# The block matrix of a linear attention loaded in two halves, and the work in a new order

## The chip, the cores and the metric

The kernel runs on one core of a Trainium2 chip. Its metric is the device time of one execution in microseconds (us). The kernel before takes 259.46 us, the median of three runs (258.75 to 259.86).

The engines have these names in the profile: PE is TensorE (PEld its loading of weights), DVE is VectorE, ACT is ScalarE, POOL is GpSimd, SP is SyncE. SPq and ACTq are the instructions with which SyncE and ScalarE issue DMAs.

## The reference

Two layers follow each other. The first is a linear attention with a feature map that takes products of two small projections; the second normalizes, and is a gated linear unit.

```
phi(x) = outer(S1 x, S2 x), flattened             # 8 x 8 = 64 features of 32 numbers
kv = sum over s of phi(k_s) v_s^T ; z = sum over s of phi(k_s)
attn = phi(q) kv / (phi(q) z + 1e-6)              # 4 batches, 4 heads, 1088 tokens, head 32
x = attn as 4352 tokens x 128
xn = x / sqrt(mean(x^2) + 1e-6) * rms_g
out = (silu(xn w_gate) * (xn w_val)) w_out        # 128 -> 1536 -> 128
```

S1, S2 and the three weights arrive as 64-bit numbers, and the kernel turns their bits into 32-bit floats itself.

## The kernel before, in words

**Stages.** S1 and S2 stand in one block matrix `sw` for the four heads, 128 x 64 numbers of 8 bytes, 64 KB. One DMA on ScalarE's queue brings it to `s_raw`. Six small instructions (lines 371 to 389: absolute value, sign, low bits, clamp, shift, join) make `sblk` of it, and each product with keys or queries needs `sblk`. Keys come by batch in two pieces, values in two or three. For a batch the kernel computes the projections of the keys (L485), copies half of each out of PSUM (L309), multiplies them to `phi` (L439) and sums `phi` times the values (L497) into `kv`. Queries come in nine chunks of up to 512 tokens. For the first two chunks the projections (L550) are multiplied token by token (tile `at`), turned by TensorE (L558) and copied to `phiq`; the later ones go through DRAM (`far`, `at`, `bt`). Then `phiq` times `kv` (L627), a division, a norm and another turn (L675) give x in two parts, `x_hi` and `x_lo`.

**Slots.** For each chunk and each of 12 slices of 128 hidden columns there is a slot: three passes for the gate and three for the value (L726, high and low parts of weights and x), silu on ScalarE (L735), product on VectorE (L738, tile `h`), its high part on ScalarE (L753), its low part on VectorE or GpSimd (L756), three passes with the output weights (L764). A slice of the weights is 384 KB, loaded at L412 and converted by lines 346 to 423 for its first use; the tiles are `w_raw`, `w_tmp`, `w_f`, `w_hi` and `w_lo`.

**Order.** Every piece of work is a task in a plan, numbered as it is added. `ORDER` is a list of all the numbers, written out, and `ON` gives, letter by letter, the engine of each task that more than one engine can do (a, d, p for ScalarE, VectorE, GpSimd). `follow` goes through `ORDER`, gives each task a planned start from clocks of its own, and `run` emits the work sorted by that planned start. A DMA that ScalarE issues has a fixed planned start (`since`) and takes nothing of SyncE's clock; a DMA without `since` takes the next place on SyncE's clock, one `ISSUE` after the one before it in the list. Within an engine the instructions run as emitted. Up to `RING` = 8 DMAs are in flight; the ninth waits on its queue for the landing of the first.

The tasks at the start, by number before the change: 0 S, 1 ScalarE's table load (a silu of four numbers), 2 to 7 the six instructions of S, 8 and 9 copies of `sblk`, 10 and 11 the first keys in two pieces (256 KB and 320.5 KB), 13 and 14 the first queries in two halves of 128 KB, 15 to 17 values, 18 to 20 the first projection of keys with its copy and product, 36 to 39 the projection of the first half of queries, its copy, its product and its turn, 41 to 44 the same for the second half. After the change S is tasks 0 and 1, and every other number is one higher.

`SLATE` is a planned delay of S's landing that the plan adds to the others.

Of the kernel before, what the change touches and what calls it, by code (L numbers as in the profile page):

```python
# [12 lines left out]
U32 = mybir.dt.uint32  # L13
# [9 lines left out]
P = 128  # L23
# [5 lines left out]
HALF = 64  # L29
# [55 lines left out]
"""  # L85
# [16 lines left out]
SWITCH = 98  # L102
RING, ISSUE, FAR, FLIGHT, SETTLE = 8, 470, 640, 1650, 250
STALLS = ((4500, 600), (12000, 400))
SLATE = 650


class Buf:
# [760 lines left out]
```

## Time and profile before

| | |
|---|---|
| median of three runs | 259.46 us |
| profiled execution, its own time | 258.33 us |
| its span (first to last instruction) | 256.5 us |
| TensorE busy | 252.0 us (98%) |
| VectorE busy | 168.6 us (66%) |
| ScalarE busy | 153.8 us (60%) |
| GpSimd busy | 90.6 us (35%) |
| granted TensorE clock | 1.00 |

A row of the chain of waits has a start, a duration (both us) and what filled it: an engine with tile and line, a DMA, or "issue". A row of the timeline begins in the same way and has the engine, the line, the operation, the tile written and the tiles read, and in brackets the idle time of the engine before it with what ended it. A row of the table by stretches has its ends, its length, and the busy time and number of instructions of PE, PEld, DVE, ACT and POOL, then the granted clock, the DMA engines' busy share and GB/s. A row of groups has a count, the busy time, the mean in ns, the idle time before them and what ended it.

### The profile page before, as it was taken

The page shows a single profiled execution, that of the slowest core. Times are in us where ns is not written, and L with a number is a line of the kernel's source. Part 1 is how long each engine was busy: PE and PEld are TensorE (multiplying, and loading weights), DVE is VectorE, ACT ScalarE, POOL GpSimd, SP SyncE. Part 2 cuts the span into 40 slices and gives each one's busy share as a digit, 9 for nine tenths or more (in the row PEclk, how much of TensorE's full clock was granted, in tenths as well). Part 3 has the DMA queues.
Part 4 walks back from the last instruction along what each step waited for, and adds up shares of the span by engine and source line. Part 5 has one row for each costly group of instructions (what it writes and reads, how often), then busy time and mean ns, then how long its engine had stood idle before and what let it go on. Part 6 is the DMA issues. An engine that isn't in the chain of part 4 may idle for free.

```text
span 256.5 us, 5598 instructions
## 1 busy us (share of the span) xinstructions
PE 252.0 (98%) x2116; PEld 204.0 (80%) x2116; DVE 168.6 (66%) x390; ACT 153.8 (60%) x339; POOL 90.6 (35%) x92
## 2 busy tenths in 40 slices
PE   7999999999999999999999999999999999999995
PEld 5888777788887787788887888888888887888895
DVE  2998999989866676646464666647644554635643
ACT  3789888647664744575555555455556655554572
POOL 3444222123755412583516503145223714132031
PEclk9999999999999999999999999999999999999999
DMA  7999886064015115061320120001000100100010
GB/s 236 380 382 279 251 236 208 0 158 130 1 59 149 65 47 139 0 185 43 92 75 3 42 78 15 0 1 43 0 0 0 41 4 0 41 0 3 0 42 20
DMA packets 13498, 22.13 MB, mean 86 GB/s; under 512 B 1952, under 2 KB 5024, under 8 KB 13472
## 3 DMA queue, kind: packets, MB, share of 16 engines
q1 hardware_dynamic: 13040, 21.52, 27.0%
q8 instruction: 16, 0.26, 0.4%
q10 hardware_dynamic: 432, 0.26, 0.3%
q14 instruction: 10, 0.08, 0.1%
HBM read 18.69 MB, written 3.08 MB: 85 GB/s over the span
## 4 chain that ended last, share of the span: by engine, by line
PE 95%; ACT 2%; DMA 1%; POOL 1%; DVE 0%; issue 0%
PE g_ps L726 28%; PE v_ps L726 28%; PE o_ps L764 28%; PE att L627 3%; PE att L497 2%; PE att L675 2%; DMA s_raw<-sw 1%; PE att L485 1%; PE att L578 1%; PE o_ps L497 1%; ACT phiq L309 0%; ACT w_tmp L362 0%; POOL at L439 0%; PE att L745 0%; PE g_ps L485 0%; PE g_ps L558 0%
## 5 line engine op out<-in xcount | busy, mean ns | idle before, releaser
L738 DVE TENSOR_TENSOR h<-v_ps,s 128x512 f32<-128x512 f32 (+2 forms) x110 | 69.9, 649 | 49.7 <-PE v_ps L726 25.7
L756 POOL TENSOR_TENSOR h_lo<-h,h_hi 128x512 fp32r<-128x512 f32 (+1 forms) x43 | 53.0, 1242 | 109.2 <-DVE h_lo L756 39.7
L735 ACT ACTIVATE s<-g_ps 128x512 f32<-128x512 f32 (+1 forms) x108 | 60.8, 574 | 39.8 <-PE g_ps L726 32.7
L753 ACT CAST h_hi<-h 128x512 fp32r<-128x512 f32 (+1 forms) x106 | 61.3, 599 | 38.6 <-DVE h L738 35.5
L756 DVE TENSOR_TENSOR h_lo<-h,h_hi 128x512 fp32r<-128x512 f32 (+1 forms) x63 | 40.8, 660 | 13.4 <-ACT h_hi L753 10.0
L726 PE MATMUL g_ps<-x_hi,w_hi 128*128 128x512 f32 (+1 forms) x110 | 42.5, 387 | 0.0
L726 PE MATMUL v_ps<-x_hi,w_hi 128*128 128x512 f32 (+1 forms) x110 | 42.3, 385 | 0.0
L726 PE MATMUL g_ps<-x_lo,w_hi 128*128 128x512 f32 (+1 forms) x110 | 41.6, 379 | 0.0
L726 PE MATMUL v_ps<-x_hi,w_lo 128*128 128x512 f32 (+1 forms) x110 | 41.6, 378 | 0.0
L726 PE MATMUL g_ps<-x_hi,w_lo 128*128 128x512 f32 (+1 forms) x110 | 41.5, 378 | 0.0
L726 PE MATMUL v_ps<-x_lo,w_hi 128*128 128x512 f32 (+1 forms) x110 | 41.5, 379 | 0.0
L764 PE MATMUL o_ps<-h_hi,w_hi 128*128 128x512 f32 (+1 forms) x106 | 41.3, 389 | 0.0
L764 PE MATMUL o_ps<-h_hi,w_lo 128*128 128x512 f32 (+1 forms) x106 | 40.7, 384 | 0.0
L764 PE MATMUL o_ps<-h_lo,w_hi 128*128 128x512 f32 (+1 forms) x106 | 40.6, 383 | 0.0
L726 PEld LDWEIGHTS g_ps<-x_hi,w_hi 128*128 128x128 f32 x110 | 20.7, 188 | 4.8 <-ACT s L735 0.2
L726 PEld LDWEIGHTS v_ps<-x_hi,w_hi 128*128 128x128 f32 x110 | 20.7, 188 | 4.6 <-DVE h L738 0.3
L726 PEld LDWEIGHTS g_ps<-x_lo,w_hi 128*128 128x128 f32 x110 | 20.7, 188 | 4.2
L726 PEld LDWEIGHTS v_ps<-x_lo,w_hi 128*128 128x128 f32 x110 | 20.6, 188 | 4.2
L726 PEld LDWEIGHTS v_ps<-x_hi,w_lo 128*128 128x128 f32 x110 | 20.7, 188 | 4.0
L726 PEld LDWEIGHTS g_ps<-x_hi,w_lo 128*128 128x128 f32 x110 | 20.7, 188 | 3.9
L764 PEld LDWEIGHTS o_ps<-h_lo,w_hi 128*128 128x128 f32 x106 | 19.9, 188 | 4.3
L764 PEld LDWEIGHTS o_ps<-h_hi,w_hi 128*128 128x128 f32 x106 | 19.9, 188 | 4.1
(97 smaller groups left out, 256.5 us busy)
## 6 DMA issues: line engine op xcount, KB each, us to landing
w_raw<-w SPq DMA_DIRECT2D x12, 384.0 KB
bt<-far SPq DMA_DIRECT2D x24, 128.0 KB
at<-far SPq DMA_DIRECT2D x12, 256.0 KB
outT<-o_sb SPq DMA_DIRECT2D x8, 256.0 KB
q<-qT SPq DMA_DIRECT2D x7, 256.0 KB
vt<-v SPq DMA_DIRECT2D x4, 272.0 KB
kt<-kT SPq DMA_DIRECT2D x4, 256.0 KB
vt<-v SPq DMA_DIRECT2D x3, 340.0 KB
```

Of the source, the lines that this page charges most:

```text
L485: nc.tensor.matmul(out=ab()[n0:rows.stop, (t - lo) * HALF:(t - lo + 1) * HALF], lhsT=kt()[:, s0:s0 + len(rows)], rhs=sblk, start=True, sto ...
L497: nc.tensor.matmul(out=kvv[r0:r0 + wide, h // 2, :], lhsT=phi()[:, t, h * F + f:h * F + f + wide], rhs=vt()[:, t, h, :], start=(t == 0 and ...
L578: nc.tensor.matmul(out=accs[p]()[a * D:(a + 1) * D, :m], lhsT=sab[rows, p].rearrange("p c o r -> p (c o r)"), rhs=q()[rows, a * m:(a + 1) ...
L627: nc.tensor.matmul(out=nv[n0:rows.stop, t, p, :], lhsT=phi()[:, p, l0:l0 + len(rows)], rhs=kvs[cut][:, p, :], start=True, stop=True,)
L675: nc.tensor.transpose(out=xt()[:, t * P:(t + 1) * P], in_=xn()[:, t, :], identity=ident)
L726: nc.tensor.matmul(out=acc()[:, cs], lhsT=wt[:, j, i3, :], rhs=x()[:, cs], start=(i == 0), stop=(i == 2))
L735: act(n, lambda: nc.scalar.activation(out=s()[:, :n], in_=gps()[:, :n], func=AF.Silu), cols(gps, whole[0]), [s])
L738: cs.stop - cs.start, lambda cs=cs: nc.vector.tensor_tensor(out=h()[:, cs], in0=vps()[:, cs], in1=s()[:, cs], op=ALU.mult),
L753: act(n, lambda: nc.scalar.copy(out=h_hi()[:, :n], in_=h()[:, :n]), hs, [h_hi], True)
L756: eng.tensor_tensor(out=h_lo()[:, :n], in0=h()[:, :n], in1=h_hi().bitcast(F32)[:, :n], op=ALU.subtract)
L764: nc.tensor.matmul(out=o_ps()[:, :n], lhsT=wt[:, j, 2, :], rhs=x()[:, :n], start=first and i == 0, stop=last and i == 2,)
```

## The change

The change was announced as "S loaded in two halves, the first transfer of both queues; both halves of the first queries by ScalarE's queue; order searched anew". S is loaded by two DMAs of 64 partitions each: the first half on SyncE's queue, planned without `since`, the second on ScalarE's with `since` 740 as before. Both halves of the first queries are now issued by ScalarE, the second one 430 ns of the plan after the first; before, the second half was SyncE's. What reads S now waits for both halves. `SLATE` becomes 250 and counts for ScalarE's half alone. `ORDER` and `ON` are replaced as a whole; below stand their first lines. Among the tasks that change the engine are the absolute value of S (2 before, 3 after: a to d) and the products of the first queries (38 and 43 before: p and d; 39 and 44 after: d and p).

```diff
 ORDER = """
-1 0 2 3 5 4 10 6 7 18 19 20 14 41 42 43 13 36 11 68 15 37 79 38 22 23 26 30 31 16 24 17 212 32 69 12 27 207 9 208 28 39 80 44 45 8 21 25 29 33 209 213
...
+1 11 2 0 3 4 6 5 7 8 19 20 14 15 12 69 21 37 38 16 80 42 39 43 17 18 23 24 31 27 44 213 208 13 32 214 9 40 25 45 28 29 22 26 33 209 210 30 34 81 215
...
 ON = (
-    "aapddadapaaapaddaaaaaappapdadpapdapdadpadpapdapdaddappappadapadddapaddaaaapdddddaadapapdaaaddddaddddddadpdddddpppdpapdda"
...
+    "dapadddapaaadaapaaaaaappappadpadpappaddaddappadpaddadpappapapadaaadaapaaaapdddddaadadapdaaadpddaddddddaddddddppdddpadapa"
...
-SLATE = 650
+SLATE = 250
...
-    plan.add({"dma": Way(
-        ISSUE + SLATE, P * NB * 8 / 320, lambda: nc.scalar.dma_start(out=s_raw.rearrange("p n c -> p (n c)"), in_=sw.bitcast(U32)), since=740
-    )}, (), ["s_raw"])
+    for i, rows in enumerate((slice(0, HALF), slice(HALF, P))):
+        eng = nc.scalar if i else nc.sync
+        plan.add({"dma": Way(ISSUE + SLATE * i, HALF * NB * 8 / 320, lambda eng=eng, rows=rows: eng.dma_start(
+            out=s_raw[rows].rearrange("p n c -> p (n c)"), in_=sw.bitcast(U32)[rows]), since=740 * i)}, (), [("s_raw", i)])
...
-    plan.add({"act": on_act(NB, s_abs, True), "dve": on_dve(NB, s_abs_dve, fast=True)}, ["s_raw", "table"], ["s_tmp"])
-    dve(NB, s_side, ["s_raw"], ["s_top"], fast=True)
-    dve(NB, s_low, ["s_raw", "s_top"], ["s_top"], lock=True)
+    plan.add({"act": on_act(NB, s_abs, True), "dve": on_dve(NB, s_abs_dve, fast=True)}, [("s_raw", 0), ("s_raw", 1), "table"], ["s_tmp"])
+    dve(NB, s_side, [("s_raw", 0), ("s_raw", 1)], ["s_top"], fast=True)
+    dve(NB, s_low, [("s_raw", 0), ("s_raw", 1), "s_top"], ["s_top"], lock=True)
...
-            eng = nc.sync if c or i else nc.scalar
+            eng = nc.sync if c else nc.scalar
             load(
                 P * (hi - lo) * 4, lambda eng=eng, lo=lo, hi=hi: eng.dma_start(out=q()[:, lo:hi], in_=qT[:, s0 + lo:s0 + hi]), [(q, i)],
-                since=0 if c or i else 1170,
+                since=0 if c else 1170 + 430 * i,
             )
```

More of the change, by code (lines that the diff above doesn't have):

```diff
@@ L48 @@
 ORDER = """
[36 rows of a table removed]
[36 rows of a table added]
 """
 ON = (
-    "aapddadapaaapaddaaaaaappapdadpapdapdadpadpapdapdaddappappadapadddapaddaaaapdddddaadapapdaaaddddaddddddadpdddddpppdpapdda"
-    "paaaadpaaadpddppdppddpaaaddaaapppddpddddppaaadpdddpdpddpddddddadadpdddpdppddppdpdpdaappaaddpppppddpdpddadpddapdpdpddpddd"
-    "dadpdddppddpa"
+    "dapadddapaaadaapaaaaaappappadpadpappaddaddappadpaddadpappapapadaaadaapaaaapdddddaadadapdaaadpddaddddddaddddddppdddpadapa"
+    "pdaaapdaddpddddppddpdpaaapddaappdpdpdpddpdaaadpadddddppppdppppdddpdaddpdppdddppddpaaddpdaddpdddddpdddpdaddpadppppdppppdp"
+    "dadpppppddpda"
 )
```

70 rows, old and new, of the table ORDER are left out of this document.

## The prediction

> **What bounds the kernel now.** I read the page's chain of work that ended last first, by engine.
>
> ```profile
> PE 95%; ACT 2%; DMA 1%; POOL 1%; DVE 0%; issue 0%
> ```
>
> TensorE is 95% of the chain. So a change can gain only where TensorE still waits (the first 18 us, as I read it, and the end) or where it changes the shape of its matrices. The chain, read again for the first 26 us, shows what TensorE waits for there:
>
> ```profile
> 0.73 3.25 DMA s_raw<-sw
> ...
> 4.01 0.27 ACT s_tmp L379
> ...
> 4.30 0.20 DVE s_tmp L382
> ...
> 4.76 0.23 DVE sblk L389
> ...
> 5.04 0.36 PE g_ps L485 x4
> ...
> 7.43 0.66 PE g_ps L558 x4
> ...
> 14.02 0.31 ACT w_hi L420
> 14.33 0.22 ACT kab L309
> ...
> 17.67 0.43 PE v_ps L726 x2
> ...
> 24.11 0.89 PE v_ps L726 x3
> 25.00 0.70 PE g_ps L726 x3
> ```
>
> S lands at 0.73 + 3.25 = 3.98 us, becomes `sblk` 1.01 us later (4.76 + 0.23), and TensorE starts at 5.04. From there the chain is computing alone, down to the last product; no later DMA stands in it. What S gains or loses is handed on whole, until something else is late. Of the other waits one bears on the change, and it stands just ahead of the 7.43: TensorE waits there for a product of GpSimd (its row comes below). The last two rows give a price that I need below: three passes of 512 columns take 0.70 us, and 0.89 straight after matrices of another shape.
>
> **The change part by part.** The sum is made against the profiled execution (258.33 us, span 256.5); the median of the runs shown, 259.46, lies 1.13 above it, and I carry the same difference over to it.
>
> *S in two halves.* The diff gives the SyncE half (task 0) no `since`, so it takes the place that the list gives it on SyncE's clock, and the new list has 11, the first keys, ahead of 0. Emission goes by planned start. The SyncE half is therefore second on its queue, behind 256 KB, whatever the words that announce the change say; only the ScalarE half is first. The second place is where half of the first queries stood:
>
> ```profile
> 0.74 0.39 SPq L457 DMA_DIRECT2D kt<-kT  x1
> 1.19 0.41 SPq L524 DMA_DIRECT2D q<-qT  x1
> ...
> kt<-kT SPq DMA_DIRECT2D x1, 320.5 KB
> ...
> kt<-kT SPq DMA_DIRECT2D x1, 256.0 KB
> ...
> q<-qT ACTq DMA_DIRECT2D x1, 128.0 KB
> ...
> s_raw<-sw ACTq DMA_DIRECT2D x1, 64.0 KB
> ```
>
> How fast the bytes move, by stretches (the last column is GB/s):
>
> ```profile
> 1.50:2.00 0.50, 0.50 (x4) 0.25 (x2) 0.00 (x0) 0.34 (x1) 0.41 (x3) 1.00 0.59 66
> 2.00:2.50 0.50, 0.50 (x4) 0.32 (x3) 0.00 (x0) 0.50 (x1) 0.00 (x0) 1.00 0.57 174
> 2.50:3.00 0.50, 0.50 (x4) 0.31 (x3) 0.00 (x0) 0.49 (x2) 0.00 (x0) 1.00 1.02 371
> 3.00:3.50 0.50, 0.50 (x4) 0.25 (x2) 0.00 (x0) 0.16 (x1) 0.00 (x0) 1.00 1.07 367
> 3.50:4.00 0.50, 0.50 (x4) 0.25 (x2) 0.00 (x0) 0.00 (x0) 0.00 (x0) 1.00 1.17 348
> 4.00:4.50 0.50, 0.34 (x2) 0.00 (x0) 0.40 (x3) 0.26 (x1) 0.00 (x0) 1.00 0.94 335
> 4.50:5.00 0.50, 0.00 (x0) 0.00 (x0) 0.45 (x3) 0.00 (x0) 0.00 (x0) 1.00 1.12 332
> ```
>
> From 2.5 us on both queues together move 371 GB/s at most, so S's landing is set by how many bytes go before its last one. Before, these were S and the first keys (320 KB, 328 thousand bytes), and up to half of SyncE's queries (64 KB). Now they are again S and the keys, and between none and all of ScalarE's first queries (128 KB), which follow its half of S. The ends: 64 KB fewer than before, 65.5/369 = -0.18 us; 128 KB more, +0.35 us. I take the middle, **+0.08**. The Trainium skill speaks against this part (DMA: Bandwidth & Descriptors, Rules for kernel authors): two transfers to disjoint halves of the partitions serialize on the same engines, and one of 128 partitions is advised. By that rule this term would be 0 and the sum below -0.31; the rows above agree with it, in that two queues at once move no more than 371 GB/s.
>
> *The absolute value goes from ScalarE to VectorE* (first letter of `ON`). VectorE's twin of it, the instruction that starts at the same 4.01, takes 0.20 where ScalarE's took 0.26:
>
> ```profile
> 4.01 0.20 DVE L371 TENSOR_SCALAR s_top<-s_raw 128x64 uint32<-128x64 uint32 x1 [3.14 <-DMA s_raw<-sw]
> ...
> 5.66 0.29 DVE L310 COPY both<-att 128x128 f32<-128x128 f32 x1 [0.67 <-PE att L550]
> 5.99 0.69 DVE L439 TENSOR_TENSOR at<-att,both 128x512 f32<-128x512 f32 x1
> 6.59 0.35 DVE L310 COPY both<-v_ps 128x192 f32<-128x192 f32 x1
> ...
> 9.99 0.36 DVE L346 TENSOR_SCALAR w_tmp<-w_tmp 128x384 f32<-128x384 f32 x1 [0.20 <-POOL at L439]
> ```
>
> The next instruction, which waited for it, starts 4.30 -> 4.23: **-0.07**, with nothing else queued on VectorE then (it had been idle for 3.14 us). ScalarE's table load moves behind one DMA issue more (0.41 us, as at 1.19), and nothing on VectorE's way waits for it.
>
> *The second half of the first queries goes to ScalarE's queue, third there.* Its issue moves from 1.19 to about 1.6 (the diff's 1170 + 430 ns), and it can become the last of five transfers: S, both pieces of keys, both halves of queries, 896.5 KB or 918 thousand bytes. By the stretches 830 thousand have moved at 4.5 us and 918 at 4.76. S came 0.74 to 0.92 us after its bytes had been counted (3.24 or 3.06 to 3.98), so this half lands at 5.50 to 5.68 at worst. The new list uses it as TensorE's third piece of work, after half of these products, at 5.21 + 0.32 = 5.53:
>
> ```profile
> 5.21 0.64 PE L550 MATMUL att<-sblk,q 128*64 128x64 f32 x16
> ```
>
>  Ends 0 and +0.18; I take **0**, since a wait there stands in front of 7.2 us, where TensorE waits today anyway. The other transfers of SyncE keep their bytes ahead of them; with eight in flight, the first weights now wait for a landing (S's first half, before 4.05) where they were issued without a wait, but the DMA share is near 1 until 5 us by the rows above, so this is covered.
>
> *The engines of the first products change places.* Before, GpSimd multiplied the half that is turned first, and TensorE waited for it; now VectorE does (tasks 39 and 44 of the new list: d, p). The wait in question, and what follows from it on GpSimd and ScalarE:
>
> ```profile
> 7.43 0.42 PEld L558 LDWEIGHTS g_ps<-ident,at 128*128 128x128 f32 x4 [0.24 <-POOL at L439]
> ...
> 8.88 1.07 POOL L439 TENSOR_TENSOR at<-both 128x512 f32<-128x512 f32 x1 [0.48 <-PE v_ps L558]
> ```
>
> VectorE's product, begun at 5.99, is done by about 6.7, so the transposes start 0.24 earlier; GpSimd's is needed only by the second of them, 0.6 later. Behind it GpSimd's next product waits for these transposes, and VectorE's conversion of weights at 9.99 for that product: the **-0.24** is handed on. Three copies leave VectorE (the rows at 5.66 and 6.59, and the second chunk's, of the form of 5.66) and one of 192 columns comes: 0.29 + 0.35 + 0.29 - 0.35 = 0.58 us less work, of which I count nothing more, because the row at 9.99 waits for GpSimd and not for VectorE's queue. At the other end those 0.58 count beyond the 0.24, another -0.34. ScalarE takes the three copies over; the wait that covers them is ScalarE's own for the first weights, and a gap ahead of it:
>
> ```profile
> 6.82 0.27 ACT L309 COPY both<-v_ps 128x128 f32<-128x128 f32 x1 [0.67 <-PE v_ps L485]
> ...
> 8.69 0.56 ACT L362 ACTIVATE w_tmp<-w_raw 128x384 f32<-128x384 f32 x1 [0.41 <-DMA w_raw<-w]
> ```
>
> Together they hold 1.08 us, against three copies of 0.27 to 0.35, 0.9 at most, which is what they would cost without this cover.
>
> *ScalarE's order to the first slots.* A copy of `kab` (0.22 on the chain) moves behind the first x. Ends 0 and -0.22 - 0.31 (with a `w_hi` as well); I take about half of the first, **-0.10**.
>
> *The order after that.* The sets of work are the same and TensorE is full in both orders. Counted in the lists, its matrices change shape 43 times where it was 42: 0 to 0.19, I take **+0.10**. Other effects of the order I price at 0 and leave to the rivals.
>
> Sum: 0.08 - 0.07 + 0 - 0.24 - 0.10 + 0.10 = **-0.23 us**: 258.1 for the profiled execution, and about **259.2** for the median.
>
> **The rivals.** *S's own half behind the keys costs more than the rest gains (slower).* S lands at +0.35, TensorE starts at 5.04 + 0.35 - 0.07 = 5.32 and waits 0.18 for the late queries. The transposes then start 0.46 after the 7.19 at which they could have started before, at 7.65 instead of 7.43: +0.22, and with the 0.10 of shapes 259.8. It decides once S lands later than about 4.3. For it: 256 KB stand ahead of this half. Against it: its place held 128 KB that nothing waited for, and S needs 32 of them.
>
> *All the early terms come whole (faster).* -0.18 - 0.07 - 0.24 - 0.34 - 0.53 = -1.36: 258.1. For it: each term has its row above. Against it: TensorE's waits in that stage depend on several engines at once, and the next one steps in.
>
> *The change does what it was announced to do*, and the SyncE half goes out first. Then 256 KB fewer are ahead of S, 262/369 = -0.71 in place of +0.08: -1.02, 258.4. Against it stand the list and the missing `since`.
>
> *VectorE falls behind between 25 and 60 us (slower).* It is nearly full there:
>
> ```profile
> 40.00:60.00 20.00, 20.00 (x251) 15.97 (x250) 18.87 (x40) 12.31 (x29) 4.76 (x5) 1.00 0.45 133
> ...
> L738 DVE TENSOR_TENSOR h<-v_ps,s 128x512 f32<-128x512 f32 (+2 forms) x110 | 69.9, 649 | 49.7 <-PE v_ps L726 25.7
> L753 ACT CAST h_hi<-h 128x512 fp32r<-128x512 f32 (+1 forms) x106 | 61.3, 599 | 38.6 <-DVE h L738 35.5
> L756 DVE TENSOR_TENSOR h_lo<-h,h_hi 128x512 fp32r<-128x512 f32 (+1 forms) x63 | 40.8, 660 | 13.4 <-ACT h_hi L753 10.0
> L354 DVE SCALAR_TENSOR_TENSOR w_tmp<-w_raw,w_tmp 128x384 uint32<-128x384 uint32 x8 | 4.4, 550 | 0.8 <-POOL w_lo L423 0.8
> ```
>
> In the new list four products of 0.70 lie between the v product of the tightest slot there (index 16) and its o product, five before. The way through h, h_hi and h_lo takes 0.65 + 0.60 + 0.66 = 1.91 us, which leaves 0.9. If VectorE runs two long and two short conversions late (0.55 twice, 0.36 twice as at 9.99: 1.82), TensorE stands for 0.9 there, and for as long again at the next weights: +1.8, 261.0. It decides once VectorE is more than 0.9 us late there. Against it: no row of this stage shows TensorE waiting now, and the list moves four of the h_lo from VectorE to GpSimd.
>
> **How the numbers follow.** Forecast 0.50 (its own range, the ends of its single terms short of all coming together, 258.7 to 259.7), all early terms 0.18, announced order of the transfers 0.05, S late 0.14, VectorE behind 0.13. A measurement of this kernel can tell about 0.5%, 1.3 us, from no change: under 258.16 is faster, over 260.76 slower. Faster takes six tenths of the second case, a third of the third and a tenth of the forecast: 0.18. Slower takes most of the last, a little of S late and of the forecast: 0.13. The rest, 0.69, is the same. The range that holds eight in ten cuts the second and the last case in two: 258.0 to 260.7.
>
> **What would show it.** The ScalarE half and the SyncE half on their queues: second place for the latter, behind kt. S's last landing near 4.05 (rival: 3.8, 4.3, or 3.3) and TensorE's first product at 5.0. The transposes at about 7.2 with no wait for GpSimd. The first slot near 17.4 where it is 17.67, and from 25 us on a TensorE without waits. I am wrong if TensorE waits anywhere between 25 and 60 us, if the first product comes before 4.7, or if the start is as I say and the end is not.

## The result, and the profile after

The changed kernel takes 261.3 us (median of 14 runs, 259.48 to 262.5); the kernel before, beside it, 258.73 us (14 runs, 258.11 to 260.09). The ratio is 1.0085, with a 95% interval of 1.0061 to 1.011: slower, by 2.2 us (1.6 to 2.8). Forecast were 259.2 us, and 258.0 to 260.7 as the range. The profiled execution took 261.33 us (span 259.5), 3.0 us more than that of before.

First the chain of work that ended last, by engine over the whole span, and then the rows of its start:

```profile
PE 95%; DMA 2%; ACT 1%; ACTq 0%; issue 0%; DVE 0%
```

```profile
2.02 5.91 DMA q<-qT
...
7.97 0.70 PE att L551 x8
8.67 1.07 PE v_ps L486 x20
9.74 0.64 PE g_ps L486 x12
10.38 0.65 PE att L551 x16
11.03 0.59 PE g_ps L559 x4
```

Before, this chain began with S (0.73 + 3.25). Now it begins with the second half of the first queries: issued at 2.02 us as ScalarE's third transfer, it lands at 7.93, where the prediction had put 5.68 as the worst. The turn of the queries (L559, L558 before) stands at 11.03 instead of 7.43.

TensorE's rows of the timeline around the wait:

```profile
5.75 0.34 PE L486 MATMUL g_ps<-sblk,kt 128*64 128x64 f32 x4 [1.15 <-DVE sblk L389]
5.91 0.40 PE L551 MATMUL att<-sblk,q 128*64 128x64 f32 x8
7.97 0.70 PE L551 MATMUL att<-sblk,q 128*64 128x64 f32 x8 [1.66 <-DMA q<-qT]
8.46 1.28 PE L486 MATMUL v_ps<-sblk,kt 128*64 128x64 f32 x20
```

TensorE starts at 5.75 (5.04 before, with S), does half of the first queries, and stands for 1.66 us. Eight products then take 0.70 where eight of the same form took 0.40 just before. The table by stretches shows why (the third column from the end is the granted clock):

```profile
5.00:7.50 2.50, 0.57 (x12) 0.43 (x12) 1.35 (x6) 0.48 (x2) 0.62 (x1) 0.95 1.01 324
7.50:10.00 2.50, 2.03 (x38) 2.03 (x40) 0.23 (x1) 0.85 (x4) 0.94 (x1) 0.50 1.04 399
10.00:12.50 2.50, 2.50 (x50) 2.27 (x46) 2.33 (x4) 1.65 (x7) 1.50 (x3) 0.87 1.03 306
...
40.00:60.00 20.00, 20.00 (x255) 15.85 (x241) 18.89 (x39) 13.58 (x34) 5.29 (x5) 1.00 0.45 121
```

The granted clock is 0.50 in the whole of the second stretch; with the shares lost in its neighbours (0.95 and 0.87) that makes about 3.4 us, from 7.25 to 10.65. From 25 us on TensorE is full again, as before. That nothing else happened later is told by the first pass of the first slot, in the timelines of before and of after:

```profile
17.60 0.38 PE L726 MATMUL v_ps<-x_hi,w_hi 128*128 128x256 f32 x1
```

```profile
20.66 0.39 PE L727 MATMUL g_ps<-x_hi,w_hi 128*128 128x256 f32 x1
```

It starts 3.06 us later, and the span is 3.0 us longer. From there to the end both take 238.9 us (256.5 - 17.60 and 259.5 - 20.66). The profiled executions of e1 and e9 below were disturbed as a whole (410 and 308 us), and only the first microseconds of their traces are read. In all other profiles the remainder is 238.7 to 239.0, so the start of the first slot measures what each execution gained or lost.

Now the transfers. The issues on the two queues, from the timeline:

```profile
0.73 0.39 SPq L458 DMA_DIRECT2D kt<-kT  x1
0.74 0.55 ACTq L393 DMA_DIRECT2D s_raw<-sw  x1
...
1.18 0.57 SPq L393 DMA_DIRECT2D s_raw<-sw  x1
...
1.33 0.60 ACTq L525 DMA_DIRECT2D q<-qT  x1
1.80 0.57 SPq L458 DMA_DIRECT2D kt<-kT  x1
...
2.02 0.47 ACTq L525 DMA_DIRECT2D q<-qT  x1
```

SyncE's half of S is second on its queue, behind the keys, as the list said. But a half of S keeps its queue for 0.55 or 0.57 us, and the transfer behind it, of the usual 128 partitions, for 0.57 or 0.60; before, these issues took 0.39 to 0.46. And the bytes come more slowly (the last column is GB/s):

```profile
3.00:3.50 0.50, 0.50 (x4) 0.25 (x2) 0.00 (x0) 0.44 (x2) 0.00 (x0) 1.00 0.67 200
3.50:4.00 0.50, 0.50 (x4) 0.25 (x2) 0.00 (x0) 0.00 (x0) 0.00 (x0) 1.00 0.45 92
4.00:4.50 0.50, 0.44 (x4) 0.09 (x2) 0.00 (x0) 0.00 (x0) 0.00 (x0) 1.00 0.61 203
```

In the same stretches 367, 348 and 335 GB/s had moved before. The DMA engines' busy share is 0.45 to 0.67: they are not full, though eight transfers are issued by 3.3 us.

The trace also holds, for each transfer, the time at which each of the 16 DMA engines reported its part done. A transfer has landed with the last. The first, the eighth and the last of these times (us):

```
                      before              after
S, ScalarE's     3.40  3.68  3.98    3.10  3.26  3.79
S, SyncE's                           3.33  3.71  4.67
keys, 1st piece  3.21  3.47  3.80    2.88  3.09  3.61
queries, 1st     3.99  4.23  4.55    3.79  4.12  5.40
queries, 2nd     3.63  4.00  4.38    5.47  5.93  7.93
keys, 2nd piece  4.78  5.05  5.58    5.20  5.74  7.75
```

Half of the engines had brought their part of the second query half by 5.93; the slowest needed 2.0 us more. The 320.5 KB of the second piece of the keys are issued ahead of this half after the change (1.80 and 2.02), where they were issued behind it before (1.65 and 1.19). The Trainium skill (DMA: Bandwidth & Descriptors, Why a DMA increments its semaphore by 16 and not by 1) says that these engines finish independently and that the semaphore counts them. The table agrees, and adds what the spread can be: 0.80 us at most in these rows of before, 2.55 in those of after.

### The profile page after: what moved, and what is told of

The parts are those of the page before. It is cut to its first block, busy times and chain, and to the rows that moved or that the text cites. A ratio compares the mean times of both kernels' runs of the same rounds, so it can differ in the third digit from the quotient of the medians.

```text
span 259.5 us, 5598 instructions
## 1 busy us (share of the span) xinstructions
PE 252.9 (97%) x2118; PEld 204.8 (79%) x2118; DVE 167.2 (64%) x386; ACT 150.8 (58%) x334; POOL 95.7 (37%) x97
## 3 DMA queue, kind: packets, MB, share of 16 engines
q1 hardware_dynamic: 12976, 21.42, 27.0%
## 4 chain that ended last, share of the span: by engine, by line
PE 95%; DMA 2%; ACT 1%; ACTq 0%; issue 0%; DVE 0%
PE v_ps L727 28%; PE g_ps L727 28%; PE o_ps L765 27%; PE att L628 3%; DMA q<-qT 2%; PE att L498 2%; PE att L676 2%; PE att L579 1%; PE att L486 1%; PE o_ps L498 1%; PE v_ps L486 1%; PE g_ps L486 1%; PE att L551 1%; PE att L746 0%; PE att L559 0%; ACTq L525 0%
## 5 line engine op out<-in xcount | busy, mean ns | idle before, releaser
L757 POOL TENSOR_TENSOR h_lo<-h,h_hi 128x512 fp32r<-128x512 f32 (+1 forms) x47 | 57.2, 1225 | 84.5 <-ACT h_hi L754 46.7
L757 DVE TENSOR_TENSOR h_lo<-h,h_hi 128x512 fp32r<-128x512 f32 (+1 forms) x59 | 38.7, 668 | 17.5 <-POOL h_lo L757 9.0
(95 smaller groups left out, 259.7 us busy)
```

The source lines that it names most:

```text
L757: eng.tensor_tensor(out=h_lo()[:, :n], in0=h()[:, :n], in1=h_hi().bitcast(F32)[:, :n], op=ALU.subtract)
```

## The experiments

Theory at first: the two places (half of S behind the keys, the second query half third on ScalarE's queue) cost what bytes ahead of them cost. Rivals: the shape of S's halves, 64 partitions, costs whatever the place; one transfer more costs, whatever its shape; TensorE's clock makes the loss; the order itself costs. The results stand here in one table. "GB/s" is that of 2.5 to 4.5 us, "slot" the start of the first slot in the profiled execution.

| kernel | median us | ratio to before, 95% | GB/s | slot |
|---|---|---|---|---|
| before | 258.57 to 259.45 | 1 | 355 | 17.60 |
| after | 261.3 | 1.0085 (1.0061 to 1.011) | 192 | 20.66 |
| e1 | 258.82 | 1.0002 (0.9987 to 1.0018) | 227 | not read |
| e2 | 259.19 | 1.0028 (1.0002 to 1.0054) | 380 | 17.65 |
| e3 | 257.74 | 0.9965 (0.995 to 0.998) | 381 | 17.33 |
| e4 | 258.71 | 1.001 (0.9985 to 1.0035) | 251 | 17.93 |
| e5 | 259.12 | 1.0 (0.9976 to 1.0025) | 346 | 20.10 |
| e6 | 260.59 | 1.0083 (1.0052 to 1.0114) | 213 | 19.19 |
| e7 | 262.31 | 1.0124 (1.0091 to 1.0156) | 223 | 21.42 |
| e8 | 257.64 | 0.9939 (0.9917 to 0.996) | 387 | 17.64 |
| e9 | 257.56 | 0.9941 (0.9917 to 0.9966) | 389 | not read |
| e11 | 258.51 | 0.9983 (0.9962 to 1.0004) | 254 | 17.46 |
| e12 | 258.79 | 0.9998 (0.9972 to 1.0023) | 356 | 18.19 |
| e13 | 258.94 | 0.9998 (0.9972 to 1.0024) | 343 | 18.42 |
| e14 | 257.89 | 0.9962 (0.9943 to 0.9981) | 380 | 16.89 |
| e15 | 258.66 | 0.9995 (0.9976 to 1.0014) | 225 | 17.99 |
| e16 | 258.6 | 0.9984 (0.9959 to 1.0009) | 300 | 18.03 |

The kernel before had medians of 258.57 to 259.45 beside these groups (its single runs gather near 258.4 and near 259.7), so kernels of different groups are compared by their ratios; 0.001 is 0.26 us.

**e1: the second query half back on SyncE's queue**, all else as after.

```diff
-            eng = nc.sync if c else nc.scalar
+            eng = nc.sync if c or i else nc.scalar
-                since=0 if c else 1170 + 430 * i,
+                since=0 if c or i else 1170,
```

> The changed kernel (261.3 us) with one part undone: the second half of the first queries is issued by SyncE again, in the third place of its queue, behind the first keys and SyncE's half of S. Theory A (the loss is the wait for this half, which came third on ScalarE's queue, landed at 7.93 us, left TensorE idle for 1.66 us and let its granted clock fall to 0.5): it lands near 4.6, TensorE's idle time there goes, the clock stays at 1.00, and the time falls by 2 us or more, to about 259. Theory B (the loss is the division of S: two queues that issue many transfers at once leave the DMA engines short between 3 and 4.5 us, and everything lands late): the GB/s stay at about 200 and 90 there, the time falls by 1 us at most, to 260.3 or more. Theory C (the new order costs): it stays at 261.

Measured: 258.82 us, ratio 1.0002. Undoing this one part gives back 0.83% (1.0085 - 1.0002), 2.1 us: the whole loss against before.

**e2: S whole on ScalarE's queue**, both query halves still on it. SyncE's task stays in the list and does nothing.

```diff
-    for i, rows in enumerate((slice(0, HALF), slice(HALF, P))):
-        eng = nc.scalar if i else nc.sync
...
+    for i in range(2):
+        plan.add({"dma": Way(ISSUE + SLATE * i, i * P * NB * 8 / 320, (lambda: nc.scalar.dma_start(
+            out=s_raw.rearrange("p n c -> p (n c)"), in_=sw.bitcast(U32))) if i else (lambda: None), since=740)}, (), [("s_raw", i)])
```

> The changed kernel with the other part undone: S comes whole, by one transfer first on ScalarE's queue; the two halves of the first queries still follow it there. Theory A: the second half of the queries lands late still (7 us or more), TensorE waits over 1 us for it, 260.5 to 261.3. Theory B: the DMA engines move over 300 GB/s from 3 to 4.5 us as before, the queries land by 5.7 and the time falls to about 259. Theory C: it stays at 261.

Measured: 259.19 us, ratio 1.0028, and 380 GB/s. So the other part, alone undone, gives back 0.57%, 1.5 us. In the profiled execution, whose 258.22 us are the lowest of the 12, the second query half still decides, but 1.9 us sooner; the chain, and TensorE's row:

```profile
1.72 4.32 DMA q<-qT
```

```profile
6.08 0.45 PE L550 MATMUL att<-sblk,q 128*64 128x64 f32 x8 [0.38 <-DMA q<-qT]
```

**e3: both undone**, which leaves the new `ORDER` and `ON` alone (the diffs of e1 and e2 together).

> The new order and the new choice of engines alone: S whole on ScalarE's queue and the second half of the first queries on SyncE's, as in the kernel before. Theories A and B: the order is worth what the prediction summed without the transfers, -0.2 to -0.4 us against the kernel before: 258.4 (ratio 0.999). Theory C: it is slower than the kernel before by 1 us or more.

Measured: 257.74 us, ratio 0.9965: the new order is faster than before by 0.35%, 0.9 us. The first slot starts at 17.33, 0.27 before that of before. In this execution TensorE waits for the second chunk's queries, and then goes straight on to the turns:

```profile
2.12 4.89 DMA q<-qT
7.05 0.69 PE att L550 x16
7.73 0.59 PE g_ps L558 x4
```

**e4: S first on both queues**, as the change was announced; task 0 goes ahead of 11 in the list.

```diff
-1 11 2 0 3 4 6 5 7 8 19 20 14 15
+1 0 11 2 3 4 6 5 7 8 19 20 14 15
```

> The changed kernel with one step in its list: SyncE's half of S goes ahead of the first keys, so that S is the first transfer of both queues, as the change was announced. Both theories A and B: S lands near 3.3 where it was 4.67, but the second half of the queries stays third on ScalarE's queue. Theory A: TensorE starts over 1 us earlier, only to wait longer for that half: the time stays within 0.5 us of the changed kernel's 261.3. Theory B: with S ahead of everything the engines are short later, and S's path gains 1 us: about 260.3. If the announced order was the point of the change: 258.4 or less.

Measured: 258.71 us, ratio 1.001. S lands at 2.73 and 3.00, but now the keys are late, and after them the second chunk's queries:

```profile
4.94 0.34 PE L486 MATMUL g_ps<-sblk,kt 128*64 128x64 f32 x4 [0.60 <-DMA kt<-kT]
...
7.62 0.69 PE L551 MATMUL att<-sblk,q 128*64 128x64 f32 x16 [0.44 <-DMA q<-qT]
```

S 1.0 us earlier than before buys 0.10 us of TensorE's start (4.94 for 5.04). The second query half is third on ScalarE's queue here too, issued at 2.03. But the second piece of the keys is issued behind it (2.25) and no longer ahead of it. The query half lands at 5.29, and TensorE does not wait for it.

**e5: S in two halves by columns**: the places, the number and the bytes of after, but each transfer has 128 partitions of 256 bytes.

```diff
-    for i, rows in enumerate((slice(0, HALF), slice(HALF, P))):
+    for i, cs in enumerate((slice(0, NB), slice(NB, 2 * NB))):
...
-            out=s_raw[rows].rearrange("p n c -> p (n c)"), in_=sw.bitcast(U32)[rows]), since=740 * i)}, (), [("s_raw", i)])
+            out=s_raw.rearrange("p n c -> p (n c)")[:, cs], in_=sw.bitcast(U32)[:, cs]), since=740 * i)}, (), [("s_raw", i)])
```

> The changed kernel with S divided by columns: each half is a transfer of 128 partitions and 256 bytes, on the same queues and in the same places. Theory shape (a transfer of 64 partitions keeps its queue for 0.55 to 0.57 us where the whole S took 0.41, its successor for 0.57 to 0.60, and the DMA engines run short from 3 to 4.5 us): the issues take about 0.41 again, the engines move 340 GB/s or more from 3 us on, and the time falls to that of the run with S whole, 259.2. Theory count (one more transfer in front is enough, whatever its shape): the engines stay at 90 to 200 GB/s in that stretch and the time at 261.

Measured: 259.12 us, ratio 1.0: 0.85%, 2.2 us, under after, and the intervals do not meet. The shape matters here. The issues are short again, and 346 GB/s move. But the profiled execution (260.8 us) still shows the second query half late, at 7.05, and the clock low behind the wait:

```profile
1.19 0.41 SPq L393 DMA_DIRECT2D s_raw<-sw  x1
...
1.72 0.39 ACTq L525 DMA_DIRECT2D q<-qT  x1
...
7.09 0.45 PE L551 MATMUL att<-sblk,q 128*64 128x64 f32 x8 [1.28 <-DMA q<-qT]
```

```profile
7.50:10.00 2.50, 2.50 (x51) 2.38 (x48) 1.44 (x3) 1.29 (x6) 2.07 (x2) 0.54 1.07 384
```

Of the 16 DMA engines eight had reported this half by 5.31 and the last at 7.05. Slow single engines are not a matter of 64 partitions alone.

**e6: TensorE kept busy during the wait**, with seven groups of products on zeros, written to an unused tile, between the two query halves.

```diff
+                    if first and u == 0:
+                        keep_warm(7, "o_ps")
```

> The changed kernel with seven small products of zeros (about 1.5 us) for TensorE between its products with the two halves of the first queries, where it waits 1.66 us for a transfer. Theory clock (part of the loss is TensorE's granted clock, 0.50 from 7.25 to 10.7 us, after that wait): the clock stays at 1.00, the 38 products of keys and queries behind the wait take 1.9 us where they took 3.06, and the time falls by 0.5 to 1.2 us, to 260.1 to 260.8. Theory data (the transfers behind, all late, set the pace): the clock stays at 1.00, and the time within 0.3 us of 261.3.

Measured: 260.59 us, ratio 1.0083, which can't be told from after. In the trace the clock is held:

```profile
7.50:10.00 2.50, 2.45 (x62) 2.19 (x61) 1.00 (x2) 1.22 (x6) 1.55 (x2) 1.00 1.02 393
```

```profile
2.01 5.56 DMA q<-qT
7.61 0.45 PE att L551 x8
8.06 0.58 PE v_ps L486 x20
8.64 0.35 PE g_ps L486 x12
8.99 0.47 PE att L551 x16
```

The four groups behind the wait take 1.85 us instead of 3.06 (0.70 + 1.07 + 0.64 + 0.65), and the first slot starts 1.47 earlier, 0.36 of which is the earlier landing. So between these two executions the low clock is worth about 1.1 us; e6's, at 259.94, is the lowest of its 12 runs. The medians differ by 0.7, the ratios by nothing. Each run lists its mean clock. Six of the 14 runs of after have the 0.993 of the profiled one, at 261.04 to 261.35 us; of the other eight, at 1.00, four took 259.48 to 260.43 and four 261.98 to 262.5. So the low clock is not the whole loss: the lowest run of after, at a listed 1.00, is above the highest of e3 (258.66). And e7, next, shows that a listed 1.00 does not prove a full clock at the start.

**e7: both halves of S on ScalarE's queue**, one behind the other, the rest as e1.

```diff
-        eng = nc.scalar if i else nc.sync
+        eng = nc.scalar
...
-            ... since=740 * i)}, (), [("s_raw", i)])
+            ... since=740 + i)}, (), [("s_raw", i)])
```

> The run with the second half of the queries on SyncE (258.82 us), with both halves of S on ScalarE's queue, one after the other, ahead of the queries; the first keys and the second half of the queries stay on SyncE's. Theory place (what delays S is that its SyncE half stands behind 256 KB of keys): S lands by 3.8 and the time falls to that of the order alone, 257.7. Theory shape (transfers of 64 partitions hold up the making of transfers on both queues): the issues of both halves and of what follows take 0.55 to 0.6 us again, the engines run short from 3 to 4.5 us, S lands near 4 and the time stays within 0.4 us of 258.8.

Measured: 262.31 us, ratio 1.0124 (6 runs), the slowest of all. S is behind no keys here, and yet its second half lands at 5.34:

```profile
6.41 0.48 PE L486 MATMUL g_ps<-sblk,kt 128*64 128x64 f32 x4 [1.42 <-DVE sblk L389]
7.16 1.12 PE L551 MATMUL att<-sblk,q 128*64 128x64 f32 x16 [0.26 <-DMA q<-qT]
```

So a half of S can be late without standing behind the keys. The late S is only part of this kernel's loss: TensorE starts 1.37 later than before, the first slot 3.82 later. Sixteen products take 1.12 us, where they took 0.64 before. That looks like a low clock from the start; the trace cannot show it, since its first record of the clock stands at 12.92 us.

**e8: S whole and first on SyncE's queue, the first keys first on ScalarE's**, with the new order and the second query half on SyncE's queue.

```diff
-1 11 2 0 3 4 6 5 7 8 19 20 14 15
+11 1 2 0 3 4 6 5 7 8 19 20 14 15
...
-        plan.add({"dma": Way(ISSUE + SLATE * i, i * P * NB * 8 / 320, (lambda: nc.scalar.dma_start(
+        plan.add({"dma": Way(ISSUE + SLATE * i, i * P * NB * 8 / 320, (lambda: nc.sync.dma_start(
...
+            eng = nc.scalar if first and not i else nc.sync
```

> A version meant to beat both: the new order with S whole and first on SyncE's queue, and the first keys first on ScalarE's. SyncE's packets have started 0.36 us before ScalarE's in the kernel before. Expected: S lands at 3.6 where it was 3.99, the first keys at about 4.1, TensorE starts at 4.7; but in the run of the order alone the chain goes through the second chunk's queries, which land at 7.0 whatever S does, so the gain against its 257.74 is between 0 and 0.4 us.

Measured: 257.64 us, ratio 0.9939: 0.61%, 1.6 us, faster than before. Against the order alone beside before (0.9965 and 0.9962) it is lower by 0.0025, and the intervals overlap. S lands at 3.60 (3.98 before), but TensorE does not start sooner, because a pair of idle products that the planner put in stands ahead:

```profile
4.40 0.59 PE att L337 x2
4.99 0.41 PE g_ps L487 x4
```

**e9: e8 without that pair**; the planner fills no gap.

```diff
-UNIT, GAP, SPARE = 226, 400, 300
+UNIT, GAP, SPARE = 226, 5000, 300
```

> The same kernel as with S first on SyncE's queue and the keys first on ScalarE's (257.64 us), but the planner fills no gap with idle products, which takes one pair of products on zeros away that stood at 4.40 to 4.99 us ahead of TensorE's first real one. Theory that TensorE's start sets the time there: the first product of queries or keys starts 0.1 to 0.3 us earlier and the time is 257.3 to 257.5. Theory that the second piece of the first keys (it landed at 6.11) or the second chunk's queries (6.71) set it: TensorE starts earlier, waits as much longer for one of the two, and the time stays at 257.6. A third way: without these products TensorE's granted clock is lower at its start, and the time is 258 or more.

Measured: 257.56 us, ratio 0.9941: the same as e8. TensorE does start sooner:

```profile
4.52 0.48 PE L487 MATMUL g_ps<-sblk,kt 128*64 128x64 f32 x4 [0.18 <-DVE sblk L389]
...
6.71 0.60 PE L487 MATMUL g_ps<-sblk,kt 128*64 128x64 f32 x12
```

In e8 this last row is

```profile
6.94 0.52 PE L487 MATMUL g_ps<-sblk,kt 128*64 128x64 f32 x12
```

Of the 0.47 us, 0.23 are left at 6.71. From 7 us on the clock of this execution is 0.75, so what becomes of the rest can't be read from it. In both kernels the first sixteen products of queries take 1.07 us, where they took 0.64 before, and the first record of the clock stands at 6.72: a low clock until then would fit, and would make an early start worth less, but it is not shown. By the times, TensorE's earlier start buys nothing. These two have the lowest ratios of the study, both below 1 with their intervals.

**e11: S by columns, the second query half on SyncE's queue** (the diffs of e1 and e5).

> The changed kernel with the second half of the first queries back on SyncE's queue, and S still in two transfers on the two queues, but each of all 128 partitions and half of the columns (256 bytes a partition) instead of 64 partitions. Theory that the shape of 64 partitions is what costs: issues of 0.39 to 0.46 us, both parts of S landed by about 4.2 us, and the time is that of the order alone with S whole, 257.7. Theory that one transfer more ahead of the others is what costs, whatever its shape: 258.8, the time of the same kernel with 64 partitions each (258.82).

Measured: 258.51 us, ratio 0.9983, between the two numbers expected. The issues are short and S lands at 4.04, but only 254 GB/s move. Neither answer holds as it stood.

**e12: the first query half by partitions.** S is whole, as in e3, and ScalarE's transfer of 128 KB is issued as two of 64 partitions.

```diff
+                    eng.dma_start(out=q()[rows, lo:hi], in_=qT[rows, s0 + lo:s0 + hi])
+                    for rows in ((slice(0, HALF), slice(HALF, P)) if cut else (slice(0, P),))
```

> The new order with S whole and the second half of the first queries on SyncE's queue (257.74 us), but ScalarE's transfer of the first half of the first queries (128 KB) is issued as two of 64 partitions each. Theory that any transfer of 64 partitions keeps its queue longer and leaves the DMA engines short: issues of 0.55 to 0.61 us in place of 0.41 to 0.46, under 300 GB/s somewhere between 3 and 4.5 us, and 258.3 to 259. Theory that it is peculiar to S, as the first transfer: issues near 0.41, and 257.7 to 257.9.

Measured: 258.79 us, ratio 0.9998, 0.33% (0.9 us) above the order alone. The issues are long here as well (0.53 and 0.60), the second part lands at 5.99, but 356 GB/s move:

```profile
1.75 4.24 DMA q<-qT
...
6.12 0.69 PE att L553 x16
```

**e13: the twin of e12, by columns**: two transfers of 128 partitions in the same places.

```diff
-                    eng.dma_start(out=q()[rows, lo:hi], in_=qT[rows, s0 + lo:s0 + hi])
-                    for rows in ((slice(0, HALF), slice(HALF, P)) if cut else (slice(0, P),))
+                    eng.dma_start(out=q()[:, u:w], in_=qT[:, s0 + u:s0 + w])
+                    for u, w in (((lo, (lo + hi) // 2), ((lo + hi) // 2, hi)) if cut else ((lo, hi),))
```

> The twin of the kernel whose first half of the first queries ScalarE issues in two transfers of 64 partitions: here they are two transfers of 128 partitions with 512 bytes each, so that number, place and bytes of the transfers are the same and the shape alone differs. Theory of the shape: ScalarE's issues take 0.41 to 0.46 us where they took 0.53 and 0.60, both parts land by 4.8 us where the last landed at 5.99, and the time is that of the order alone, 0.9965 of before, 257.7. Theory of the count (one transfer more costs, whatever its shape): the last part lands after 5.5 us, and the time is that of its twin, 1.000 of before.

Measured: 258.94 us, ratio 0.9998, the same as its twin. For this transfer the shape theory falls: the issues are short (0.94 for two), and the last part lands no sooner, at 6.69:

```profile
1.17 0.94 ACTq L525 DMA_DIRECT2D q<-qT  x2
...
6.73 0.57 PE L553 MATMUL att<-sblk,q 128*64 128x64 f32 x12 [1.41 <-DMA q<-qT]
```

Eight DMA engines had reported it by 5.27, twelve by 5.64, and the last four by 5.99, 6.26, 6.41 and 6.69. Behind this wait of 1.41 us TensorE keeps its clock: twenty products take 0.58 us, where they took 1.07 behind the 1.66 of after.

**e14, e15 and e16: e3, e1 and e11 once more, side by side**, without an edit.

> The new order alone, with S whole and the second half of the first queries on SyncE's queue, once more, as the common base for the two kernels beside it: 0.9965 of before, and more than 320 GB/s from 3 to 4.5 us.

> The changed kernel with the second half of the first queries back on SyncE's queue, S in halves of 64 partitions, once more for a profile that can be read and for a comparison on one chip. Theory of the shape: about 1.0 us above the order alone; issues of S of 0.55 and 0.60, S's second half landed after 4.1 us and the queries after 5.1, under 200 GB/s in a part of 3 to 4.5 us. Theory of the count: the same time as with S by columns, within 0.3 us.

> S by columns in the same places, once more. Theory of the shape: 0.3 us or less above the order alone and at least 0.4 below the halves by partitions beside it; if the 90 GB/s at 4 us belonged to one execution, more than 300 there now. Theory of the count: the same time as the halves by partitions, within 0.3 us, and about 100 GB/s at 4 us again.

Measured: 257.89, 258.66 and 258.6 us. The order alone is faster again (0.9962). The halves by partitions and by columns are 0.06 us apart, so with these transfers in these places it is the extra transfer that costs (0.7 to 0.8 us by these medians), and its shape makes no difference that can be told. The rates are 380, 225 and 300 GB/s (381, 227 and 254 the first time): a lower rate for S by partitions belongs to the kernel, and it alone does not make the time. In e15 the chain goes through the second piece of the keys, in e14 through S and no other transfer:

```profile
2.42 4.49 DMA kt<-kT
...
6.96 0.45 PE v_ps L486 x8
```

```profile
0.73 3.15 DMA s_raw<-sw
...
5.68 0.72 PE v_ps L485 x20
```

**Taken together**, in per cent of before: the order -0.35 (e3) and -0.38 (e14). Over the order alone:

| what is added to the order | kernels | per cent |
|---|---|---|
| one transfer more among the first, by partitions or by columns, of S or of queries | e1, e11, e12, e13, e15, e16 | +0.2 to +0.4 |
| of these, S by partitions | e1, e15 | +0.37, +0.33 |
| the second query half third on ScalarE's queue, S whole | e2 | +0.63 |
| both, S by partitions | after | +1.20 |
| both, S by columns | e5 | +0.35 |
| both, S by partitions and first on both queues | e4 | +0.45 |
| S by partitions, both halves on ScalarE's queue | e7 | +1.6 |

The two parts of after, measured one at a time, add up to +1.00, and +1.20 was measured together, with an interval of about 0.25 to either side: the loss of after is about their sum. Three kernels do not fit such a sum. In e4 the second piece of the keys stands behind the second query half and not ahead of it, which the trace shows; in e7 TensorE's products are slow as well. Why columns cost so much less than partitions in e5, and not in e16, is not settled; nor is why single DMA engines fall behind when more transfers are in flight early. That they do is shown by the times at which they report.

## Why the prediction was wrong, step by step

*Right.* SyncE's half is second on its queue, behind the keys. The absolute value on VectorE: the six instructions take 0.92 us from the first to the end of `sblk` (4.77 to 5.69), against 0.98 before (4.01 to 4.99): -0.06 where -0.07 was said. No wait from 25 us on: the rival of VectorE behind fell (row 40 to 60 us above). That the announced order of the transfers is not what the kernel does was right too; its price was not: -1.02 was said for S first on both queues, and e4 can't be told from before (1.001); in its trace the keys are late instead, and the second query half stood third there as well.

*The step that failed* is the second half of the first queries on ScalarE's queue: "lands at 5.50 to 5.68 at worst", ends 0 and +0.18, taken at 0. It landed at 7.93, and TensorE stood 1.66 us for it. (The 0.18 itself has no working: 5.68 - 5.53 is 0.15.) e1 undoes this part alone, and the loss against before is gone. Alone over the order, with S whole, it costs 0.63%, 1.6 us (e2). Two assumptions in the step were wrong. It counted bytes and let them flow as before, at 355 GB/s from 2.5 to 4.5 us; they flowed at 192. And it took one landing time for a transfer, where there are 16: eight engines were done by 5.93, near the bound, and the last came 2.0 us later. That the same place on the queue need not be late is shown by e4 (5.29), where fewer bytes stood ahead. I had the spread of before in my own number (0.74 to 0.92 us between the count of S's bytes and its landing) and carried it over as if it were fixed.

*The term for S* was taken at +0.08, ends -0.18 and +0.35. In the profile of after S lands 0.69 later (3.98 to 4.67), outside the ends. In three other executions with the same two halves in the same places it lands at 3.92 (e6), 4.10 (e1) and 4.15 (e15), -0.06 to +0.17, inside. The size of this term changes from one execution to the next, by the slowest engine; the mean of the four is +0.23. But the halves cost more than S's own landing: +0.37 and +0.33% over the order (e1, e15), about 0.9 us where the term had 0.08. In e15 the chain goes through the keys and not through S, so the term left out what the halves do to the transfers behind them.

*The rival "S late"* had the right sign, and its condition held in the profiled execution: S landed at 4.67, after its 4.3, and TensorE started at 5.75. But the chain does not go through S. The wait for the late queries ended last, and the rival had priced it at 0.18.

*The base of the sum* was three runs of before, with a median of 259.46; 14 runs have 258.73. On that base the forecast of -0.23 is 258.5, and the miss is 2.8 us and not 2.1.

*The clock* was in no term. The rows of after (0.50 after the wait) and of e6 (1.00) show it, worth about 1.1 us between two executions. The Trainium skill (TensorE: Matmul & The Clock Gate, Part 1: The HAM clock gate) says that an idle window of about 3.4 us, which runs freely, halves the clock; the 0.50 agrees. The 3.4 us for which it lasted agree too. But TensorE was not idle for a whole window: in the 3.4 us before the fall it worked for about 1.3 us (until 4.60, and from 5.75 to 6.31). Waits of 1.15 and 1.66 us were enough in after, waits of 0.46 and 1.28 in e5, and one of 1.41 was not in e13.

*The order*: with -0.24 for the turns, -0.10 for ScalarE, +0.10 for shapes and -0.07 for the absolute value I had -0.31 together. The order alone, these four included, measured -0.9 to -1.0 us. So the gain was larger than forecast, nearer to the case of all early terms (-1.36). The turns themselves stand at 7.73 in e3 and at 7.29 in e14 (7.43 before, 7.2 forecast): whether the 0.24 appears hangs on when the second chunk's queries land.

*The rule of the Trainium skill* that the prediction weighed, one transfer of 128 partitions instead of two of disjoint halves, was the better guide, and I used it for S's term alone, by its reason, that the two serialize. By that reason a second transfer costs nothing; here one transfer more cost 0.2 to 0.4% in six kernels, by partitions or by columns.

## What to carry to other kernels

A transfer lands when its slowest DMA engine is done, so a bound from bytes over rate holds for the typical engine only; when more or smaller transfers are put in flight early, allow for a last engine 1 to 2 us late, and look at what waits for that transfer first. A transfer that TensorE needs as its third piece of work is better not issued behind a large one that is needed later: here 320.5 KB ahead of it or behind it went with a landing at 7.93 or at 5.29. A start that waits for several transfers is not made faster by speeding up one of them: S a microsecond earlier bought 0.1. Try an order and a change of transfers apart: here the order gained 0.9 us and the transfers with which it came lost 3.1.

## What I had not expected of the hardware

A transfer of 64 partitions keeps its queue 0.53 to 0.61 us, and one of 128 partitions behind it on that queue 0.57 to 0.61 (0.81 once, in e4), against 0.39 to 0.47 for the others in the first 3.3 us of after. In e7 one on the other queue took 0.57 as well. With S in two such halves 192 to 251 GB/s move from 2.5 to 4.5 us in six profiles, with S by columns 254 to 346 in three, with S whole 343 to 389 in eight. The 16 engines end one transfer within 0.4 us of each other in one execution (the second piece of the keys in e3: 4.97 to 5.33) and within 2.6 in another (after: 5.20 to 7.75).
